# Masking ahead of the exponential: a top-k attention and two gated layers on one core

## The chip, the cores and the metric

The kernel runs on one NeuronCore of a Trainium2 chip. The metric is the device time of one execution in microseconds. Five engines share the work: PE (TensorE, matrix products), DVE (VectorE), ACT (ScalarE), POOL (GpSimd) and SP (SyncE, which here only issues DMAs). Each runs its own list of instructions strictly in order, and semaphores join the lists.

## The reference

The input is q, k and v of 4 batches x 8 heads x 576 tokens x 64, and four weight matrices of 512 x 2048 or 2048 x 512, which come as 64-bit floats.

```
scores = q @ k^T / 8                                  # 576 x 576 for each head
kth    = the 32nd largest score of each row
scores = where(scores >= kth, scores, -1e9)
attn   = exp(scores - max(scores)); attn = attn / (sum(attn) + 1e-9)
x      = attn @ v, heads side by side                 # 2304 tokens x 512
h      = max(x @ w_in1, 0);  y = (h * h) @ w_out1
h      = y @ w_in2;          out = (h * clip(h + 3, 0, 6) / 6) @ w_out2
```

## The kernel before, in words

Matrix operands are split into two 16-bit halves, a high and a low one, and a product is the sum of three 16-bit products (high-high, high-low, low-high). So most steps come as a pair: ACT copies the high half, POOL or DVE subtracts it to get the low half.

**Attention.** The queries of a batch are cut into blocks: four of 128 tokens, and one of 64 whose heads go in pairs. A block has 8 tiles (one for a head), the short one 4, 144 in all. In `attend` a tile goes through: `qk` on PE (128 x 576 scores in PSUM); `evac`, ACT, to `S` in SBUF; `topk`, seven instructions on DVE: MAX8 gives the 8 largest of a row, MATCH_REPLACE8 strikes them out into a copy `W`, and so on, until `m` holds the 32 largest; `bias` on POOL (scale times the maximum, negated); `expo` on ACT, `E` = exp(scale * S + bias), which needs only the first MAX8; `mask` on DVE, one instruction that multiplies `E` by (S >= 32nd value) and also adds up the row; `high` on ACT and `low` on POOL, which fill `wc`; `flip`, a DMA transpose from `wc` to `wT`, issued by SP; `av` on PE, which multiplies `wT` with the values.

**From a block to a unit.** When a block's tiles are done, `x_operand` divides by the row sums, transposes on PE and splits the result into the operand buffer `hl`. A unit is 128 tokens (a full block, or two short ones): 18 units. For each, `group` runs eight steps for either layer: 4 x 12 products into `hb` (`up`), ACT and DVE for the nonlinearity, ACT `high` and POOL `low` into `ghl`, then products into `acc`. The second layer of a unit needs all of its first layer.

**Weights.** SP loads 67 pieces of the four matrices; DVE turns the 64-bit words into 32-bit floats (`conv`), ACT and POOL add low bits, PE and DVE find a scale from the whole matrix (`gram`, `maxes`), and PE, ACT and POOL split the scaled pieces. The first layer's products wait for the scales and pieces of matrices 0 and 1.

**What sets the order.** `Plan` holds every step as a task with an engine, a cost in microseconds, a key, its predecessors and the buffers it takes. It plays the program through: an engine that is free takes the ready task with the lowest key whose buffers are free; a task's successors become ready its cost plus a latency later (`LAT`; 2.0 for SP). The order in which tasks start there is the order of each engine's instructions. Keys are pairs: a class, then a position. The classes are the constants at the end of the file: `AKEY` (attention on ACT and POOL), `GKEY` (the layers on ACT and POOL), `CKEY`, `WKEY`, `SKEY`, `SPL` (weights), `XKEY`, `PREP`, `QKV`. Buffer counts are the numbers given to `pool`.

Of the kernel before, what the change touches and what calls it, by code (L numbers as in the profile page):

```python
# [32 lines left out]
class Plan:  # L33
# [99 lines left out]
def tile_topk_attention_moe_moe2(  # L133
# [79 lines left out]
    acc_t = ps.tile([P, 2, 512], F32, name="acc")  # L213
    plan.pool(acc0=1, acc1=1)
    pool("S", SBUFS, [P, S], F32)
    pool("W", 2, [P, S], F32)
    pool("E", 2, [P, S], F32)
    pool("wc", 2, [P, 2 * S], F16)
    pool("wT", 2, [P, 2 * S // P, P], F16)
# [17 lines left out]
    scalar("wmx", 4)
# [349 lines left out]
    def norm_tasks(tag, src, junk, n, cost, deps, alloc, inv, kkey, reads=(), writes=()):  # L587

        box = {}

        def square():
            for a_ in alloc:
                T[a_, kkey] = take(a_)
            box["ss"] = take("ss")
            nc.scalar.activation(junk(), src(), AF.Square, accum_out=box["ss"][0:n])

        def total():
            box["pn"] = take("misc", "pn" + tag)
# [88 lines left out]
    def q_prep(i, half):  # L687
# [63 lines left out]
    def attend(s):  # L751
# [87 lines left out]
        for r in range(7):  # L839
# [8 lines left out]
        tm = task("DVE", 0.815, (2, s + 0.7), mask, port=True, deps=[ops[6], te, mask_task.get((i, 0))],  # L848
                  alloc=["sums"] if t == 0 else [])
        mask_task[i, t] = tm  # L850
        free("S", tb, tm)
        free("m", ops[0], tm)
        th = task("ACT", 0.57, (AKEY[2], s), high, deps=[tm, before[2]], alloc=["wc"])
        tl = task("POOL", 1.38, (AKEY[3], s), low, deps=[th, before[3]])
        free("E", te, tl)
# [425 lines left out]
SPL = (3.5, 1.5, 0.5)
ADD = (0.5, 1)
PREP = 1.5
VKEY = 3

CKEY = ((-3.61, 0.14), (-69.99, 3.36), (-31.64, 0.91), (-0.36, 1.29))
SKEY = (0, 100, 200, 300)
# [27 lines left out]
```

## Time and profile before

| | |
|---|---|
| median of 3 runs | 1236.63 us (1236.08 to 1240.48) |
| the profiled execution | 1238.58 us, span 1236.8 us, 36708 instructions |
| PE busy | 1074.3 us, 87% of the span |
| DVE busy | 1058.9 us, 86% |
| ACT busy | 825.4 us, 67% |
| POOL busy | 663.8 us, 54% |
| granted TensorE clock, mean | 0.947 |

The span runs from the first instruction to the last; the 1.8 us by which the execution is longer lie around it. Busy time is the union of an engine's instructions. An instruction's mean duration includes its way through the engine, and the next one may start before it ends; so what an instruction costs its engine is best read from start to start, where a timeline shows it.

### The profile page before, as it was taken

To read this page: it belongs to the slowest core of one execution; us is meant where nothing else is said; L and a number is where in the kernel's file an instruction comes from. 1 tells how busy PE (TensorE), PEld (TensorE's weight loads), DVE (VectorE), ACT (ScalarE), POOL (GpSimd) and SP (SyncE) were. 2 spreads that over 40 slices of the span, in tenths; PEclk is the share of its full clock that TensorE was granted. 3 is DMA by queue.
4 is the path that set the end of the run, shared out by engine and by line. 5 is a ranking of instruction groups with operands and counts; after the bars stand their busy time and mean duration, and the time that the engine had idled before them with its cause. 6 is when DMAs were issued, how large, how long until landed. Compare 5 with 4: busy or idle time off the path is not lost.

```text
span 1236.8 us, 36708 instructions
## 1 busy us (share of the span) xinstructions
PE 1074.3 (87%) x14856; PEld 879.4 (71%) x14856; DVE 1058.9 (86%) x2463; ACT 825.4 (67%) x1580; POOL 663.8 (54%) x969
## 2 busy tenths in 40 slices
PE   2484389878989999999899999999998999999998
PEld 2332147577679769877887888788767868978885
DVE  5999999999978999999999999999868989999011
ACT  7677588769767668666766757576866666755422
POOL 5857846458654556554545555655544555545312
PEclk9676599998999999999899999999998999999999
DMA  9989744333454233344574323435433233433100
GB/s 209 268 247 265 228 101 115 71 55 55 96 113 93 53 63 70 66 71 82 89 109 72 68 56 71 55 64 98 97 59 73 54 66 73 65 49 58 22 2 18
DMA packets 276762, 112.47 MB, mean 91 GB/s; under 512 B 257521, under 2 KB 265713, under 8 KB 276593
## 3 DMA queue, kind: packets, MB, share of 16 engines
q1 hardware_dynamic: 276592, 110.14, 43.3%
q8 instruction: 116, 1.90, 0.6%
q14 instruction: 54, 0.43, 0.1%
HBM read 48.23 MB, written 4.72 MB: 43 GB/s over the span
## 4 chain that ended last, share of the span: by engine, by line
PE 42%; DVE 15%; ACT 10%; DMA 10%; issue 5%; POOL 5%; SPq 1%; POOLq 0%; DVEq 0%; ACTq 0%
PE hb L1075 16%; PE acc L1118 9%; PE acc L1110 8%; DMA wT<-wc 8%; DVE W L783 4%; DVE m L786 4%; PE av L829 3%; PE sp L764 3%; DVE E L801 2%; DVE m L778 2%; POOL wc L810 1%; ACT E L795 1%; POOL ghl L1100 1%; ACT x L896 1%; ACT S L770 1%
## 5 line engine op out<-in xcount | busy, mean ns | idle before, releaser
L1075 PE MATMUL hb<-hl,w 128*128 128x128 f16 x6912 | 455.8, 220 | 3.7 <-ACT r L1082 2.2
L1075 PEld LDWEIGHTS <-w 128*128 128x128 f16 x6912 | 415.7, 99 | 42.8 <-issue 6.2
L786 DVE MAX8 m<-W 128x8 f32<-128x576 f32 x432 | 314.8, 747 | 0.2
L1100 POOL TENSOR_TENSOR ghl<-r,ghl 128x512 f16<-128x512 f32 x144 | 172.7, 1201 | 193.3 <-ACT ghl L1097 141.9
L1110 PE MATMUL acc<-ghl,w 128*128 128x128 f16 x3456 | 242.0, 221 | 9.9 <-POOL ghl L1100 4.2
L810 POOL TENSOR_TENSOR wc<-E,wc 128x512 f16<-128x512 f32 x144 | 167.8, 1165 | 145.2 <-ACT wc L806 117.8
L1118 PE MATMUL acc<-w,ghl 128*128 128x512 f16 x864 | 234.3, 382 | 2.8 <-POOL ghl L1100 1.5
L1110 PEld LDWEIGHTS <-w 128*128 128x128 f16 x3456 | 212.8, 99 | 29.8 <-issue 14.0
L783 DVE MATCH_REPLACE8 W<-m,W 128x576 f32<-128x576 f32 x288 | 213.3, 742 | 0.0
L795 ACT ACTIVATE E<-S,scalars,scl 128x576 f32<-128x576 f32 x144 | 124.8, 867 | 85.9 <-POOL scalars L790 65.3
L801 DVE SCALAR_TENSOR_TENSOR E<-S,m,E 128x576 f32<-128x576 f32 x144 | 137.2, 952 | 0.1
L770 ACT ACTIVATE S<-sp 128x576 f32<-128x576 f32 x144 | 92.9, 645 | 53.8 <-DVE E L801 40.9
L764 PE MATMUL sp<-kT,qT 128*128 128x288 f16 (+1 forms) x640 | 102.4, 303 | 25.0 <-ACT S L770 21.0
L829 PE MATMUL av<-vv,wT 128*128 128x64 f16 (+1 forms) x2240 | 92.7, 197 | 33.7 <-DMA wT<-wc 32.8
L829 PEld LDWEIGHTS <-wT 128*128 128x128 f16 (+1 forms) x2240 | 81.2, 103 | 56.5 <-DMA wT<-wc 46.9
L1097 ACT ACTIVATE ghl<-r 128x512 f16<-128x512 f32 x144 | 89.8, 626 | 40.9 <-PE acc L1110 21.2
L778 DVE MAX8 m<-S 128x8 f32<-128x576 f32 x144 | 107.3, 746 | 4.9 <-ACT S L770 4.9
L783 DVE MATCH_REPLACE8 W<-m,S 128x576 f32<-128x576 f32 x144 | 106.8, 741 | 0.0
L1118 PEld LDWEIGHTS <-ghl 128*128 128x128 f16 x864 | 73.8, 99 | 45.2 <-issue 3.3
L806 ACT ACTIVATE wc<-E 128x576 f16<-128x576 f32 x144 | 97.7, 679 | 4.6 <-DVE E L801 4.5
L412 POOL TENSOR_TENSOR w<-w,stg 128x512 int32<-128x512 int32 x57 | 73.0, 1294 | 35.4 <-DVE w L365 23.6
L1090 DVE SCALAR_TENSOR_TENSOR r<-r,hb 128x512 f32<-128x512 f32 x72 | 48.9, 680 | 49.6 <-ACT r L1084 49.4
(128 smaller groups left out, 1343.2 us busy)
## 6 DMA issues: line engine op xcount, KB each, us to landing
w<-in_moe_w_in_dram SPq DMA_DIRECT2D x32, 512.0 KB, 4.8
w<-in_moe_w_out_dram SPq DMA_DIRECT2D x29, 512.0 KB, 4.8
out_dram<-o SPq DMA_DIRECT2D x16, 256.0 KB, 2.4
qf<-in_q_dram SPq DMA_DIRECT2D x31, 128.0 KB, 3.1
stg<-in_k_dram SPq DMA_DIRECT2D x12, 256.0 KB, 3.2
stg<-in_v_dram SPq DMA_DIRECT2D x12, 256.0 KB, 3.1
wT<-wc SPq DMA_TRANSPOSE x144, 3.2
stg<-in_moe_w_out_dram SPq DMA_DIRECT2D x6, 256.0 KB, 3.9
```

The source lines that it names most:

```text
L764: nc.tensor.matmul(dst, qT[:, 2 * ((2 * hp + hh) % 4) + a, 0:M], kflat[:, hh * SPAD + c * HALF:hh * SPAD + (c + 1) * HALF], start=a == 0, ...
L778: nc.vector.max(m[:, 0:8], T["S", s])
L783: nc.vector.match_replace(out=T["W", s], in_to_replace=m[:, 8 * c - 8:8 * c], in_values=T["S", s] if c == 1 else T["W", s], imm_value=-3.0e38)
L786: nc.vector.max(m[:, 4 * r:4 * r + 8], T["W", s])
L795: nc.scalar.activation(T["E", s], T["S", s], AF.Exp, bias=T["nb", s], scale=T["scl", ("q", i, half)][:, hp % 2:hp % 2 + 1])
L801: nc.vector.scalar_tensor_tensor(T["E", s], T["S", s], T["m", s][:, TOPK - 1:TOPK], T["E", s], op0=ALU.is_ge, op1=ALU.mult, accum_out=T["s ...
L810: nc.gpsimd.tensor_tensor(wc[:, S + TAIL:], e[:, 0:S - TAIL], wc[:, 0:S - TAIL], op=ALU.subtract)
L829: nc.tensor.matmul(out_[cols, t * D:(t + 1) * D], wT[0:kr, a, cols], vv[0:kr, vb, hh, c, :], start=n_ == 0, stop=n_ == len(prods) - 1)
L1075: nc.tensor.matmul(box["h"][:, fi * n:(fi + 1) * n], wt[2 * m][:, kk * 4 + f // 4, a, f % 4 * P:(f % 4 + 1) * P], hl[:, c, kk, 0:n], start ...
L1100: nc.gpsimd.tensor_tensor(flat(box["g"][:, 1]), flat(box["r"]), flat(box["g"][:, 0]), op=ALU.subtract)
L1110: nc.tensor.matmul(flat_[:, c * w_:c * w_ + n], wt[1][:, f, a, c * P:(c + 1) * P], gl[d], start=(f, a, d) == (0, 0, 0) and c * w_ % 512 == ...
L1118: nc.tensor.matmul(o_, gl[d][:, ch * P:ch * P + rows], wt[3][:, f, a, :], start=f == 0 and (a, d) == (0, 0), stop=f == KF - 1 and (a, d) = ...
```

## The change

The mask moves. After `topk`, DVE computes one value for each row, `kb` = 32nd value x 2^96. ACT then writes `E` = relu(kb - 2^96 * S), which is zero for a kept score and huge for another. POOL subtracts, `E` = S - E. The exponential runs on `E` and adds up the row itself (`accum_out`). DVE's masking instruction is gone. `S` is now freed by POOL's subtraction, `E` is held from the relu to `low`, and the exponential waits for the whole of `topk`. The factor 1/8 moves into the q scale, and `scl` is bounded from below.

The buffers: `W` 2 to 1, `m` 3 to 4, `nb` 2 to 3, `hl` from 2 of 256 columns to 4 of 128 (the same bytes). SP's transposes of `wc` get a planned latency of 3.5 us instead of 2.0. Nearly all keys get new numbers; the layers' classes on ACT and POOL go from 4 and 1.5 to 29.26 and 27.97, which is behind the attention's.

```diff
-    pool("W", 2, [P, S], F32)
+    pool("W", 1, [P, S], F32)
-    pool("hl", 2, [P, 2, KD, 2 * P], F16)
+    pool("hl", HBUFS, [P, 2, KD, P], F16)
-    pool("m", 3, [P, TOPK], F32, st)
+    pool("m", 4, [P, TOPK], F32, st)
...
+        def lowest():
+            T["kb", s] = take("kb")
+            nc.vector.tensor_scalar(T["kb", s], T["m", s][:, TOPK - 1:TOPK], FAR, None, op0=ALU.mult)
+        def below():
+            T["E", s] = take("E")
+            nc.scalar.activation(T["E", s], T["S", s], AF.Relu, bias=T["kb", s], scale=-FAR)
+        def mask():
+            nc.gpsimd.tensor_tensor(T["E", s], T["S", s], T["E", s], op=ALU.subtract)
         def expo():
-            T["E", s] = take("E")
-            nc.scalar.activation(T["E", s], T["S", s], AF.Exp, bias=T["nb", s],
-                                 scale=T["scl", ("q", i, half)][:, hp % 2:hp % 2 + 1])
-        def mask():
             if t == 0:
                 T["sums", i] = take("sums")
-            nc.vector.scalar_tensor_tensor(T["E", s], T["S", s], T["m", s][:, TOPK - 1:TOPK], T["E", s],
-                                           op0=ALU.is_ge, op1=ALU.mult, accum_out=T["sums", i][:, t:t + 1])
+            nc.scalar.activation(T["E", s], T["E", s], AF.Exp, bias=T["nb", s],
+                                 scale=T["scl", ("q", i, half)][:, hp % 2:hp % 2 + 1],
+                                 accum_out=T["sums", i][:, t:t + 1])
...
-        te = task("ACT", 0.76, (AKEY[1], s), expo, deps=[tn, before[1]], alloc=["E"])
+        tk = task("DVE", 0.07, (2, s + 0.7), lowest, deps=[ops[6]], alloc=["kb"])
+        tr = task("ACT", 0.68, (AKEY[1], s), below, deps=[tk, before[1]], alloc=["E"])
+        tm = task("POOL", 1.24, (MKEY, s), mask, deps=[tr])
+        free("S", tb, tm)
+        te = task("ACT", 0.96, (AKEY[1], s), expo, deps=[tn, tm, mask_task.get((i, 0))], ...)
-        tm = task("DVE", 0.815, (2, s + 0.7), mask, port=True, deps=[ops[6], te, mask_task.get((i, 0))], ...)
-        tw = task("SP", 1.25, (0, s), flip, deps=[tl, before[4]], alloc=["wT"])
+        tw = task("SP", 1.25, (0, s), flip, deps=[tl, before[4]], alloc=["wT"], lat=WLAT)
...
-GKEY = (4, 1.5)
-AKEY = (0.5, 1, 3, 3.5)
+GKEY = (29.26, 27.97)
+AKEY = (0.09, 1, 4.41, 4.29)
-WKEY = ((45.68, 1), (153.74, 0.1), (14.48, 0.1), (62.46, 0.1))
+WKEY = ((36.97, 0.2), (83.47, 1.54), (106.39, 0.2), (97.4, 0.05))
```

On DVE, in the middle of the program, two tiles took turns in the top-k steps before (the numbers behind W and m are one tile's buffers):

```order
L783 MATCH_REPLACE W_10658<-m_10625,S_10361 128x576
L783 MATCH_REPLACE W_10486<-m_10359,W_10486 128x576
L786 MAX m_10625<-W_10658 128x8
L786 MAX m_10359<-W_10486 128x8
L783 MATCH_REPLACE W_10658<-m_10625,W_10658 128x576
L1090 SCALAR_TENSOR_TENSOR r_10687<-r_10687,hb_10547 128x512
L801 SCALAR_TENSOR_TENSOR E_10457,sums_10319<-S_10252,m_10359,E_10457 128x576
```

Now, at about the same tile, one tile goes through alone, and line 795 stands for the mask:

```order
L795 TENSOR_SCALAR scalars_85<-m_10291 128x1
L783 MATCH_REPLACE W_10656<-m_10485,S_10440 128x576
L786 MAX m_10485<-W_10656 128x8
L783 MATCH_REPLACE W_10656<-m_10485,W_10656 128x576
L1101 SCALAR_TENSOR_TENSOR r_10690<-r_10690,hb_10525 128x512
L786 MAX m_10485<-W_10656 128x8
L783 MATCH_REPLACE W_10656<-m_10485,W_10656 128x576
L786 MAX m_10485<-W_10656 128x8
```

With one `W`, an instruction of DVE now mostly reads what the one just ahead of it wrote. In the whole list, DVE has 12 such neighbours among the top-k steps and what follows them before, and 503 now: 232 times a MAX behind its own MATCH_REPLACE (6 before), 184 times a MATCH_REPLACE behind its own MAX (5 before), 87 times line 795 behind its own MAX.

On POOL, a stretch in the second half of the program before (wc is a tile's low half, ghl that of a layer's step):

```order
L790 TENSOR_SCALAR scalars_85<-m_11415,scl_10321 128x1
L279 TENSOR_TENSOR kn_11346<-qf_10988,kn_11346 128x4x64
L810 TENSOR_TENSOR wc_11413<-E_11195,wc_11413 128x512
L811 TENSOR_TENSOR wc_11413<-E_11195,wc_11413 128x64
L279 TENSOR_TENSOR kn_11346<-qf_10988,kn_11346 128x4x64
L1100 TENSOR_TENSOR ghl_11510<-r_11475,ghl_11510 128x512
L1100 TENSOR_TENSOR ghl_11570<-r_11526,ghl_11570 128x512
```

And a like stretch now:

```order
L803 TENSOR_TENSOR E_11630<-S_11345,E_11630 128x576
L966 TENSOR_TENSOR hl_11481<-y_11551,hl_11481 128x512
L1111 TENSOR_TENSOR ghl_11677<-r_11646,ghl_11677 128x512
L790 TENSOR_SCALAR scalars_85<-m_11719,scl_10844 128x1
L818 TENSOR_TENSOR wc_11737<-E_11630,wc_11737 128x512
L819 TENSOR_TENSOR wc_11737<-E_11630,wc_11737 128x64
L803 TENSOR_TENSOR E_11773<-S_11463,E_11773 128x576
```

Each tile has one more wide instruction on POOL (line 803), which stands between the steps of the layers; the low half of a tile comes four rows behind its own subtraction, with ACT's exponential and copy in between.

On SP, the loads around the last pieces of matrix 1 (in_moe_w_out) before, where matrix 2 (in_moe2_w_in) and 3 (in_moe2_w_out) are mixed in:

```order
L343 DMA w3_89<-in_moe2_w_in_dram 128x1024 x2
L343 DMA w2_88<-in_moe_w_out_dram 128x1024
L725 DMA_TRANSPOSE qT_960<-kn_959 128x8x128
L343 DMA w3_89<-in_moe2_w_in_dram 128x1024 x2
L703 DMA qf_1094<-in_q_dram 128x4x64
L343 DMA w3_89<-in_moe2_w_out_dram 128x1024
L343 DMA w2_88<-in_moe_w_out_dram 128x1024 x2
L343 DMA w3_89<-in_moe2_w_out_dram 128x1024
```

And now:

```order
L343 DMA w2_88<-in_moe_w_out_dram 128x1024 x3
L823 DMA_TRANSPOSE wT_859<-wc_815 128x9x128
L343 DMA w2_88<-in_moe_w_out_dram 128x1024 x2
L823 DMA_TRANSPOSE wT_905<-wc_882 128x9x128
L343 DMA w3_89<-in_moe2_w_in_dram 128x1024
L343 DMA w2_88<-in_moe_w_out_dram 128x1024
L343 DMA w3_89<-in_moe2_w_in_dram 128x1024
L823 DMA_TRANSPOSE wT_1001<-wc_964 128x9x128
L343 DMA w3_89<-in_moe2_w_in_dram 128x1024 x4
```

The last piece of matrix 1 was the 50th weight load of SP and is now the 33rd; pieces of matrices 2 and 3 moved behind it.

## Rows read from the trace of the kernel before

**Rows 1.** The page: busy us of each engine, share of the span, instructions

```profile
PE 1074.3 (87%) x14856; PEld 879.4 (71%) x14856; DVE 1058.9 (86%) x2463; ACT 825.4 (67%) x1580; POOL 663.8 (54%) x969
```

**Rows 2.** Busy time by stretch: length, then each engine, granted clock, DMA share, GB/s

```profile
0.00:180.00 180.00, 93.83 (x546) 53.15 (x547) 157.25 (x340) 125.34 (x233) 118.56 (x146) 0.75 0.82 225
180.00:300.00 120.00, 101.40 (x1384) 83.08 (x1382) 115.33 (x273) 95.48 (x184) 69.97 (x104) 0.94 0.39 74
300.00:1150.00 850.00, 798.99 (x11857) 678.06 (x11855) 776.59 (x1828) 574.02 (x1110) 456.19 (x703) 0.98 0.41 73
1150.00:1237.00 87.00, 80.12 (x1080) 65.08 (x1078) 9.69 (x25) 30.51 (x55) 19.05 (x18) 0.99 0.04 12
```

**Rows 3.** PE's waits, 300 to 1237 us: in total, times, longest

```profile
PE av L829 <- DMA wT<-wc: 26.6, 25, 2.3
```

**Rows 4.** The tile wT: its transposes from issue to landing

```profile
DMA to landing us min/median/max: 3.2/3.2/5.1
```

**Rows 5.** DVE's mask, line 801, by stretch; the group of a 128x1 instruction

```profile
0.00:1237.00 1237.00, 138.34 (x288) 0.95 0.44 91
...
300.00:1150.00 850.00, 111.38 (x230) 0.98 0.41 73
...
L262 DVE TENSOR_SCALAR scalars<-scalars 128x1 int32<-128x1 int32 x114 | 17.5, 153 | 4.2
```

**Rows 6.** Timeline of DVE, the last tile alone: start us, duration us, instruction

```profile
1138.68 0.80 DVE L801 SCALAR_TENSOR_TENSOR E<-S,m,E 128x576 f32<-128x576 f32 x1
...
1139.48 0.74 DVE L783 MATCH_REPLACE8 W<-m,W 128x576 f32<-128x576 f32 x1
1140.26 0.76 DVE L786 MAX8 m<-W 128x8 f32<-128x576 f32 x1
...
1141.13 0.74 DVE L783 MATCH_REPLACE8 W<-m,W 128x576 f32<-128x576 f32 x1
1141.91 0.76 DVE L786 MAX8 m<-W 128x8 f32<-128x576 f32 x1
1142.78 0.82 DVE L801 SCALAR_TENSOR_TENSOR E<-S,m,E 128x576 f32<-128x576 f32 x1
```

**Rows 7.** Timeline of DVE, two tiles in turn

```profile
1031.92 0.74 DVE L786 MAX8 m<-W 128x8 f32<-128x576 f32 x1
...
1032.64 0.74 DVE L783 MATCH_REPLACE8 W<-m,S 128x576 f32<-128x576 f32 x1
1033.30 0.08 DVE L783 MATCH_VALUE_LOAD W<-m,W 128x8 f32 x1
```

**Rows 8.** Groups of ACT and POOL: busy us, mean ns, idle before

```profile
L810 POOL TENSOR_TENSOR wc<-E,wc 128x512 f16<-128x512 f32 x144 | 167.8, 1165 | 145.2 <-ACT wc L806 117.8 <-DVE m L778 15.3 <-issue 5.6
L795 ACT ACTIVATE E<-S,scalars,scl 128x576 f32<-128x576 f32 x144 | 124.8, 867 | 85.9 <-POOL scalars L790 65.3 <-POOL wc L811 20.3
L806 ACT ACTIVATE wc<-E 128x576 f16<-128x576 f32 x144 | 97.7, 679 | 4.6 <-DVE E L801 4.5
L412 POOL TENSOR_TENSOR w<-w,stg 128x512 int32<-128x512 int32 x57 | 73.0, 1294 | 35.4 <-DVE w L365 23.6 <-ACT stg L408 6.1 <-DVE scalars L466 2.3
L811 POOL TENSOR_TENSOR wc<-E,wc 128x64 f16<-128x64 f32 x144 | 50.2, 349 | 0.0
L595 ACT ACTIVATION_READ_ACCUMULATOR kn<-qf 128x1 f32 (+1 forms) x39 | 7.6, 194 | 0.0
```

**Rows 9.** Timeline of DVE: matrix 1's maximum; the last block's row sums

```profile
145.39 0.68 DVE L362 TENSOR_SCALAR cv<-w 128x512 int32<-128x512 int32 x1
145.99 0.68 DVE L365 SCALAR_TENSOR_TENSOR w<-w,cv 128x512 int32<-128x512 int32 x1
146.58 0.68 DVE L448 TENSOR_REDUCE scalars<-acc 128x1 f32<-128x512 f32 x1
...
1143.64 0.17 DVE L880 TENSOR_SCALAR rv<-sums 128x8 f32<-128x8 f32 x1
```

**Rows 10.** Timeline of PE: the first product of the layers

```profile
179.41 0.83 PE L1075 MATMUL hb<-hl,w 128*128 128x128 f16 x12
```

More of the change, by code (lines that the diff above doesn't have):

```diff
@@ L215, in tile_topk_attention_moe_moe2 @@
     pool("S", SBUFS, [P, S], F32)
-    pool("W", 2, [P, S], F32)
+    pool("W", 1, [P, S], F32)
     pool("E", 2, [P, S], F32)
     pool("wc", 2, [P, 2 * S], F16)
-    pool("wT", 2, [P, 2 * S // P, P], F16)
+    pool("wT", WTB, [P, 2 * S // P, P], F16)
     pool("kn", 1, [P, 4 * NCH * D], F16)
@@ L233, in tile_topk_attention_moe_moe2 @@
     pool("scl", 3, [P, 2], F32, st)
-    for name, n in (("nb", 2), ("ss", 6), ("sck", 1), ("scv", 1), ("scq", 2), ("qinv", 2), ("xy", 2), ("scx", 6),
+    for name, n in (("nb", NBUFS), ("kb", 2), ("ss", 6), ("sck", 1), ("scv", 1), ("scq", 2), ("qinv", 2), ("xy", 2), ("scx", 6),
                     ("px", 6), ("sc2", 4), ("p2", 2), ("r", 6), ("pm", 2), ("sm", 2), ("ca", 2), ("oc", 2)):
@@ L602, in scale @@
             box["sc"] = take("sc" + tag)
-            scale_pair(box["pn"][:, 0:1], inv(), EXP_I, box["sc"])
+            scale_pair(box["pn"][:, 0:1], inv(), EXP_I - (3 << 23) * (tag == "q"), box["sc"])
         t1 = task("ACT", cost, (PREP, when(kkey)), square, deps=deps, alloc=["ss", *alloc], reads=reads, writes=writes)
@@ L721, in scales @@
                 nc.gpsimd.tensor_scalar(T["scl", kkey][:, c:c + 1], kvinv[:, 0, b % 2, hp:hp + 1],
-                                        T["qinv", kkey][:, 0:1], 0.125, op0=ALU.mult, op1=ALU.mult)
+                                        T["qinv", kkey][:, 0:1], SCLMIN, op0=ALU.mult, op1=ALU.max)
         def flip():
@@ L844, in attend @@
         tn = task("POOL", 0.25, (0, s), bias, deps=[ops[0], scl_use[i, half][0]], alloc=["nb"])
-        te = task("ACT", 0.76, (AKEY[1], s), expo, deps=[tn, before[1]], alloc=["E"])
+        tk = task("DVE", 0.07, (2, s + 0.7), lowest, deps=[ops[6]], alloc=["kb"])
+        free("m", ops[0], tk, tn)
+        tr = task("ACT", 0.68, (AKEY[1], s), below, deps=[tk, before[1]], alloc=["E"])
+        free("kb", tk, tr)
+        tm = task("POOL", 1.24, (MKEY, s), mask, deps=[tr])
+        free("S", tb, tm)
+        te = task("ACT", 0.96, (AKEY[1], s), expo, deps=[tn, tm, mask_task.get((i, 0))],
+                  alloc=["sums"] if t == 0 else [])
         free("nb", tn, te)
         scl_use[i, half][1].append(te)
[L848 to L853, printed above, removed]
+        mask_task[i, t] = te
+        th = task("ACT", 0.57, (AKEY[2], s), high, deps=[te, before[2]], alloc=["wc"])
         tl = task("POOL", 1.38, (AKEY[3], s), low, deps=[th, before[3]])
-        free("E", te, tl)
-        tw = task("SP", 1.25, (0, s), flip, deps=[tl, before[4]], alloc=["wT"])
+        free("E", tr, tl)
+        tw = task("SP", 1.25, (0, s), flip, deps=[tl, before[4]], alloc=["wT"], lat=WLAT)
         free("wc", th, tw)
@@ L860, in attend @@
         av_tasks[i, t] = tv
-        tile_tasks.append((ta, te, th, tl, tw, tv))
+        tile_tasks.append((ta, tr, th, tl, tw, tv))
         free("wT", tw, tv)
@@ L1265 @@
 XBUFS = 1
+HBUFS = 4
 GBUFS = 3
@@ L1271 @@
 SQ0 = 'a'
-GKEY = (4, 1.5)
-AKEY = (0.5, 1, 3, 3.5)
+GKEY = (29.26, 27.97)
+AKEY = (0.09, 1, 4.41, 4.29)
 SX = 'a'
 SX0 = 'a'
-XKEY = 1.5
+XKEY = 37.4
 NPOOL = (4, 4, 4, 4)
-QKV = 0
-WKEY = ((45.68, 1), (153.74, 0.1), (14.48, 0.1), (62.46, 0.1))
+QKV = 4.45
+WKEY = ((36.97, 0.2), (83.47, 1.54), (106.39, 0.2), (97.4, 0.05))
 SPE = ('eeee', 'eeee', 'eeea', 'aaaa')
[L1281 to L1287, printed above, removed]
+SPL = (2.26, 0.06, 0.05)
+ADD = (-0.97, 0.86)
+PREP = 1.04
+VKEY = 27.33
+MKEY = -0.5
+WLAT = 3.5
+WTB = 2
+NBUFS = 3
+FAR = 2.0 ** 96
+SCLMIN = 2.0 ** -56
+CKEY = ((-3.23, 0.38), (-66.39, 4.6), (-35.42, 1.77), (-0.72, 1.02))
+SKEY = (0.99, 124.56, 208.36, 272.85)
 _INS = ["q", "k", "v", "moe_w_in", "moe_w_out", "moe2_w_in", "moe2_w_out"]
```

## The prediction

> **What bounds the kernel now.** I read the busy times first: PE 87%, DVE 86%, ACT 67%, POOL 54% [rows 1]. Two engines are nearly full and the other two have room; the change takes work from one of the full ones and gives it to the two with room. Then the stretches [rows 2], since an average hides stages. From 0 to 180 us PE is busy 93.8 us, so 86.2 are idle: this is the stage of weights, with DVE at 157.3 of 180 and DMA at 0.82. The layers' first product starts at 179.4 [rows 10], 33 us behind the maximum of matrix 1 at 146.6 [rows 9]. From 180 to 300, PE's idle time is 18.6 us; from 300 to 1150 it is 51.0 with DVE at 776.6 of 850 (91%); in the last 87 us it is 6.9 and DVE has nothing left. These four make 162.7, and 1074.3 + 162.7 = 1237. So there are two limits at once: PE must do its 1074 us, and DVE must finish the last block (1143.6, [rows 9]) before the last 93 us can run. Third, PE's waits: in the 57.9 us that PE is idle after 300, 26.6 are one wait, `av` for the transposed `wT` [rows 3]. A transpose takes 3.2 to 5.1 us to land [rows 4], and the plan of before counts 2.0, so its order puts `av` a little too early, 25 times.
>
> **DVE: the mask goes.** Line 801 holds DVE for 138.3 us, its accumulator reads included [rows 5], of which a part overlaps the next instruction: undisturbed it is 0.73 + 0.07 us from start to the next work (1138.68 to 1139.48, [rows 6]), 144 x 0.80 = 115. I take 127, between the two.
>
> **DVE: line 795 comes.** 144 instructions on one value a row. A like one is 153 ns long [rows 5], so 22 us is the upper end; pipelined behind independent work it would be about half. I take 10; zero is the lower end.
>
> **DVE: one `W`.** With two tiles in turn, MATCH_REPLACE8 to the next instruction is 0.66 us (1032.64 to 1033.30) and MAX8 to the MATCH_REPLACE8 proper 0.72 (1031.92 to 1032.64) [rows 7]. In the one tile that ran alone at the end these are 0.78 (1139.48 to 1140.26) and 0.87 (1140.26 to 1141.13), and MAX8 to the mask, which reads its result, 0.87 against 0.66 [rows 6]. So an instruction that reads what its neighbour has just written costs 0.12, 0.15 or 0.21 us more. The new order has 226, 179 and 86 more such neighbours: 226 x 0.12 + 179 x 0.15 + 86 x 0.21 = 27 + 27 + 18 = 72 us. This is the price of the buffer that the change gives up, and it shows nowhere in DVE's busy time. Its lower end is zero, if other waits cover it; its upper end is 503 x 0.21 = 106. DVE's net is thus -127 + 10 + 72 = -45 us, with ends -138 and +13 (-115 + 22 + 106).
>
> The Trainium skill says otherwise here: on its page "VectorE: DVE Perf Modes", section "The DRAIN you can't avoid", a chain of VectorE instructions costs the same with a semaphore after each as with one after the last. This trace disagrees, by the 0.12 to 0.21 us above. By that rule the 72 us would not be there and DVE's net would be -117; that is a rival below.
>
> **ACT.** The relu over 128x576 is new. Its neighbours are the copy of line 806 (679 ns, no operand per row) and the exponential of line 795 before (867 ns, two such operands) [rows 8]; relu has one, so 0.77, and 144 x 0.77 = 111 us, ends 98 and 125. The exponential's sum adds an accumulator read of 194 ns [rows 8]: 28 us. Together 139: ACT goes from 825 to about 964, 80% of a span of 1206. From 300 to 1150 there are 115 tiles (230 instructions of line 801, two for a tile, [rows 5]), one in 7.4 us: 574 + 115 x 0.96 = 684 of 850, 81%. There is room, but queues get longer. From 180 to 300 ACT already has 95.5 of 120 [rows 2]; 0.96 us for each of 16 tiles make it 111, 92%. There ACT is nearly the bound, and I charge 2 us of PE idle time to it.
>
> **POOL.** The subtraction is 576 wide. From the low half of 512 columns (1165 ns) it would be 1.31 us, from the 32-bit addition of line 412 (1294 ns) 1.46 [rows 8]. 144 x 1.31 = 189, ends 168 (no more than the 512 columns cost) and 210. POOL goes from 664 to about 853, 71%. Neither engine becomes the bound by its sum.
>
> **PE.** Its instructions are the same in number and kind. What changes is when they can run.
> First stage: ahead of the maximum of matrix 1, DVE has 20 conversion steps fewer (0.68 us long, about 0.6 from start to start [rows 9]: -12), 9 masks fewer (-8), and pays some 28 neighbour stalls (+4); so the maximum comes about 15 us sooner on DVE's account, and the matrix's last piece is SP's 33rd load and not the 50th. But the split that follows runs on ACT, which has more to do ahead of it: one more tile of evacuation and nine relus and sums. I count 8 us of gain, ends 20 and -4.
> After 300: the plan now waits 3.5 us for a transpose. In the new order the layers' products that stand between a tile's `qk` and its `av` are worth some 34 us of PE's work, counted over all tiles, and not 32. The chain behind top-k grows by about 3 us (relu, subtraction and exponential 0.77 + 1.31 + 1.06 come, the mask's 0.8 goes, two hand-overs more), while a tile alone is through DVE's seven steps in 4 x 0.66 + 3 x 0.72 + 3 x 0.12 + 3 x 0.15 = 5.6 us, and two in turn take 9.6 for both. So `av` has 2 - 3 + 4 = 3 us more room, and I let 22 of the 26.6 us go. Four `hl` buffers instead of two let the attention run further ahead of the layers, which covers some of the small gaps; from the other 31 us I take 3. The rest stays.
> Sum on PE's side: 1074.3 busy + (86.2 - 8) + (18.6 + 2) + (57.9 - 25) = 1206.
>
> DVE's side must agree: 1143.6 - 45 = 1099 for the last block. Behind the last `av`, PE has 768 + 336 products of 128 columns left and not 636 + 288 as before, 1.19 times as many; the last 87 us with 80.1 busy [rows 2] become about 87 + 15 = 102, plus the 6 between the row sums and that window. 1099 + 108 = 1207. The two sides meet within a microsecond, so neither is slack, and I forecast a span of 1206. The execution is 1.8 us longer than its span and the profiled run lies 2.0 above the median of before (1238.58 against 1236.63), so as a median 1206.
>
> **Rivals.**
> First, slower: the two `E` buffers. Before, `E` is held over the exponential, mask, copy and low half. Now it is held over relu 0.77, subtraction 1.31, exponential 0.87 + 0.19, copy 0.68 and low half 1.17 + 0.35 = 5.3 us of work [rows 8] plus five hand-overs between ACT and POOL, each behind whatever stands in line. 850 us for 115 tiles is 7.4 us a tile, so two buffers allow a hold of 14.8: 1.9 us per hand-over. At 2.0 us, the hold is 15.3 and a tile takes 7.65: 0.25 x 115 = 29 us more, and with 8 gained early 1237 + 29 - 8 = 1258. For it: ACT at 81% and POOL at 71%, each with instructions of about a microsecond in line, and the layers' work now stands last in their classes, so that PE starves first. Against it: the waits on `ghl` are small today and POOL idles 145 us ahead of line 810 [rows 8].
> Second, nothing happens: DVE's stalls and line 795 come at their upper ends, the net is about zero, the last block stays at 1143, and PE's saved waits for `wT` only turn into waits for the next block. With 4 us from the first stage this is 1233. For it: the bounds above include it.
> Third, no stall between neighbours, as if rows 6 held for the program's end alone. DVE's net is -117, DVE ends at about 1027 and is no limit any more. PE keeps 75 + 16 us idle before 300 and, with its wait on `wT` and half of the rest gone, 16 after: 1074.3 + 107 = 1181. For it: little but that rows 6 are few; against it, all three kinds of neighbours in [rows 6] show the stall.
> The Trainium skill's section named above would have this rival too; the trace is against it, by [rows 6].
>
> **How the numbers follow.** 0.5% of 1236.6 is 6.2 us, so faster means below 1230, slower above 1243. The forecast, 1192 to 1222 on its own: chance 0.60, all faster. The third rival 0.13, faster. The second 0.13: most within 0.5%, 0.03 of it below 1230. The first 0.14, of which 0.01 ends within 0.5%. That makes faster 0.76, same 0.11, slower 0.13. The range of 1176 to 1243 leaves out the first rival and the far end of the third.
>
> **What would show it.** DVE's busy time falls to about 945 while its last block ends only some 45 us sooner; from start to start its top-k steps read 0.78 and 0.87. ACT near 964 and POOL near 853. PE's wait for `wT` after 300 falls below 8 us. Matrix 1's maximum comes before 140 and the first product before 175. Wrong would be: PE's waits for `ghl` or `hb` of tens of microseconds, relus that wait for line 819 (the first rival), a DVE without stalls that ends before 1050 (the third), or a last block at 1140 (the second).

## The result, and the profile after

The changed kernel takes 1205.74 us (median of 4 runs, 1203.63 to 1206.85) against 1238.56 (4 runs, 1236.08 to 1240.84): a ratio of 0.9733, 95% interval 0.9706 to 0.9761. The profiled execution took 1205.79 us, its span 1204.0, the mean granted clock of TensorE 0.968 (0.947 before). That difference in clock is not the gain: 17 further executions of the kernel before, with a granted clock of 0.964 to 0.967, have a median of 1235.9 us, less than 3 us below 1238.56. The prediction was 1206, faster.

The page's busy times, which answer to [rows 1]:

```profile
PE 1072.1 (89%) x14856; PEld 879.2 (73%) x14856; DVE 991.3 (82%) x2319; ACT 929.2 (77%) x1868; POOL 833.8 (69%) x1113
```

DVE has 68 us less, ACT 104 more, POOL 170 more. The same four stretches as in [rows 2]; the last is shorter, since the program is:

```profile
0.00:180.00 180.00, 106.56 (x632) 59.86 (x633) 152.98 (x344) 139.68 (x273) 133.27 (x163) 0.90 0.74 210
180.00:300.00 120.00, 94.53 (x1259) 77.09 (x1258) 112.11 (x264) 101.47 (x205) 91.52 (x119) 0.90 0.44 97
300.00:1150.00 850.00, 824.46 (x12424) 707.85 (x12424) 719.84 (x1700) 674.25 (x1370) 599.24 (x824) 0.99 0.40 74
1150.00:1204.00 54.00, 46.55 (x546) 34.42 (x543) 6.33 (x13) 13.80 (x22) 9.81 (x10) 0.99 0.03 11
```

Length less PE's busy time is PE's idle time: 73.4 us in the first stage (86.2 before), 25.5 in the second (18.6), and 25.5 + 7.5 = 33.0 after 300 (57.7 before, to the end of its span at 1236.8). 1072.1 + 131.9 = 1204. PE's waits after 300 us, the longest sum and the one of [rows 3]:

```profile
PE sp L764 <- ACT S L770: 8.9, 14, 4.6
...
PE av L837 <- DMA wT<-wc: 1.5, 3, 0.8
```

The 25 waits for a transpose have become three. Now DVE, one tile alone in mid-program, which answers to [rows 6] and [rows 7] (start us, duration us, instruction):

```profile
1005.43 0.74 DVE L786 MAX8 m<-W 128x8 f32<-128x576 f32 x1
1006.21 0.15 DVE L795 TENSOR_SCALAR scalars<-m 128x1 f32<-128x1 f32 x1
1006.28 0.08 DVE L783 MATCH_VALUE_LOAD W<-m,S 128x8 f32 x1
1006.35 0.74 DVE L783 MATCH_REPLACE8 W<-m,S 128x576 f32<-128x576 f32 x1
1007.13 0.76 DVE L786 MAX8 m<-W 128x8 f32<-128x576 f32 x1
1007.92 0.09 DVE L783 MATCH_VALUE_LOAD W<-m,W 128x8 f32 x1
1008.00 0.74 DVE L783 MATCH_REPLACE8 W<-m,W 128x576 f32<-128x576 f32 x1
1008.78 0.76 DVE L786 MAX8 m<-W 128x8 f32<-128x576 f32 x1
```

From start to start, MATCH_REPLACE8 to its own MAX8 is 0.78 us (1006.35 to 1007.13), MAX8 to its own MATCH_REPLACE8 0.87 (1007.13 to 1008.00), MAX8 to line 795 0.78 (1005.43 to 1006.21). The groups that the change made, with line 818 as the old line 810 (busy us, mean ns, idle before; [rows 8]):

```profile
L803 POOL TENSOR_TENSOR E<-S,E 128x576 f32<-128x576 f32 x144 | 203.7, 1415 | 42.6 <-ACT E L800 41.6 <-PE av L837 0.5
L818 POOL TENSOR_TENSOR wc<-E,wc 128x512 f16<-128x512 f32 x144 | 167.9, 1166 | 55.5 <-ACT wc L814 54.7
```
```profile
L808 ACT ACTIVATE E<-E,scalars,scl 128x576 f32<-128x576 f32 x144 | 124.2, 863 | 2.9 <-POOL E L803 2.8
...
L808 ACT ACTIVATION_READ_ACCUMULATOR E<-E,scalars,scl 128x1 f32 x144 | 28.1, 195 | 0.0
...
L795 DVE TENSOR_SCALAR scalars<-m 128x1 f32<-128x1 f32 x144 | 21.5, 149 | 3.0
```

The new relu of line 800 stands beside them at 774 ns. Last the three marks: on DVE the maximum of matrix 1 and the last block's row sums [rows 9], on PE the first product of the layers [rows 10]:

```profile
128.16 0.69 DVE L448 TENSOR_REDUCE scalars<-acc 128x1 f32<-128x512 f32 x1 [0.23 <-PE acc L428]
...
1091.24 0.15 DVE L795 TENSOR_SCALAR scalars<-m 128x1 f32<-128x1 f32 x1
...
1095.02 0.17 DVE L891 TENSOR_SCALAR rv<-sums 128x8 f32<-128x8 f32 x1
1095.23 0.20 DVE L892 RECIPROCAL rv<-rv 128x8 f32<-128x8 f32 x1
```
```profile
166.05 0.83 PE L1086 MATMUL hb<-hl,w 128*128 128x128 f16 x12 [0.21 <-DVE w L365]
```

The row sums now come from ACT: DVE's own part of the last block is over with line 795 at 1091.4, and the mark at 1095 stands 3.6 us behind it. Before, DVE wrote the sums itself, and the mark followed at once.

### The profile page after: what moved, and what is told of

Its sections match the earlier page's. It is cut to its first block, busy times and chain, and to the rows that moved or that the text cites. A ratio compares the mean times of both kernels' runs of the same rounds, so it can differ in the third digit from the quotient of the medians.

```text
span 1204.0 us, 37051 instructions
## 1 busy us (share of the span) xinstructions
PE 1072.1 (89%) x14856; PEld 879.2 (73%) x14856; DVE 991.3 (82%) x2319; ACT 929.2 (77%) x1868; POOL 833.8 (69%) x1113
## 4 chain that ended last, share of the span: by engine, by line
PE 39%; DVE 22%; ACT 17%; POOL 11%; issue 5%; DMA 4%; SPq 1%; POOLq 0%; ACTq 0%; DVEq 0%
PE hb L1086 15%; PE acc L1129 10%; PE acc L1121 7%; DVE W L783 6%; DVE m L786 6%; POOL E L803 4%; PE sp L764 3%; DVE m L778 2%; POOL wc L818 2%; ACT E L808 2%; ACT S L770 2%; PE av L837 2%; ACT x L907 1%; ACT E L800 1%; DVE cv L362 1%
## 5 line engine op out<-in xcount | busy, mean ns | idle before, releaser
L1086 PE MATMUL hb<-hl,w 128*128 128x128 f16 x6912 | 461.3, 220 | 3.7 <-DVE r L1101 1.1
L786 DVE MAX8 m<-W 128x8 f32<-128x576 f32 x432 | 325.9, 754 | 7.9
L1111 POOL TENSOR_TENSOR ghl<-r,ghl 128x512 f16<-128x512 f32 x144 | 166.9, 1161 | 120.5 <-ACT ghl L1108 112.8
L803 POOL TENSOR_TENSOR E<-S,E 128x576 f32<-128x576 f32 x144 | 203.7, 1415 | 42.6 <-ACT E L800 41.6
L1121 PEld LDWEIGHTS <-w 128*128 128x128 f16 x3456 | 211.2, 99 | 18.2 <-issue 4.8
L818 POOL TENSOR_TENSOR wc<-E,wc 128x512 f16<-128x512 f32 x144 | 167.9, 1166 | 55.5 <-ACT wc L814 54.7
L800 ACT ACTIVATE E<-S,scalars 128x576 f32<-128x576 f32 x144 | 111.5, 774 | 28.4 <-DVE scalars L795 27.3
L808 ACT ACTIVATE E<-E,scalars,scl 128x576 f32<-128x576 f32 x144 | 124.2, 863 | 2.9 <-POOL E L803 2.8
L1129 PEld LDWEIGHTS <-ghl 128*128 128x128 f16 x864 | 73.8, 98 | 46.7 <-issue 5.5
L764 PEld LDWEIGHTS <-qT 128*128 128x128 f16 (+1 forms) x640 | 56.9, 105 | 61.6 <-issue 40.9
L1095 ACT ACTIVATE r<-hb,bias,scalars 128x512 f32<-128x512 f32 x72 | 55.8, 775 | 54.1 <-PE hb L1086 52.3
```

What stands on the lines that cost most here:

```text
L764: nc.tensor.matmul(dst, qT[:, 2 * ((2 * hp + hh) % 4) + a, 0:M], kflat[:, hh * SPAD + c * HALF:hh * SPAD + (c + 1) * HALF], start=a == 0, ...
L786: nc.vector.max(m[:, 4 * r:4 * r + 8], T["W", s])
L800: nc.scalar.activation(T["E", s], T["S", s], AF.Relu, bias=T["kb", s], scale=-FAR)
L803: nc.gpsimd.tensor_tensor(T["E", s], T["S", s], T["E", s], op=ALU.subtract)
L808: nc.scalar.activation(T["E", s], T["E", s], AF.Exp, bias=T["nb", s], scale=T["scl", ("q", i, half)][:, hp % 2:hp % 2 + 1], accum_out=T["s ...
L818: nc.gpsimd.tensor_tensor(wc[:, S + TAIL:], e[:, 0:S - TAIL], wc[:, 0:S - TAIL], op=ALU.subtract)
```

## The experiments

A number that comes out right doesn't show that its reasons were. The prediction's theory was two limits at once: PE's work with its waits, and DVE's end. The rivals: PE alone decides, with what it waits for, and DVE's relief does little; the new order of the weights and layers does it, not the mask; and, after the first results, the fit of the plan: how well one particular order happens to mesh.

In the table below, idle is PE's, by stretch; the last block is the start of RECIPROCAL for its row sums. Ratios are to the kernel before on the same chip (1237.2, 1238.2 and 1237.6 us in the three groups of runs). PE's busy time differs by up to 18 us between the runs, though all have the same number of products, 14,856; so PE's time does not divide cleanly into busy and idle.

| kernel | us | ratio (95%) | PE busy | idle 0-180, 180-300, after | last block | first layer product |
|---|---|---|---|---|---|---|
| before | 1238.6 | 1 | 1074.3 | 86.2, 18.6, 57.7 | 1143.8 | 179.4 |
| after | 1205.7 | 0.973 (0.971-0.976) | 1072.1 | 73.4, 25.5, 33.0 | 1095.2 | 166.1 |
| old_plan_latency | 1229.3 | 0.994 (0.991-0.996) | 1070.4 | 94.4, 16.3, 46.2 | 1133.7 | 225.3 |
| old_mask_moved | 1247.8 | 1.008 (1.005-1.011) | 1080.4 | 84.1, 31.7, 49.9 | 1113.8 | 224.6 |
| new_mask_on_dve | 1232.9 | 0.996 (0.994-0.998) | 1086.8 | 71.4, 22.3, 50.4 | 1131.5 | 155.6 |
| new_two_w | 1225.8 | 0.991 (0.987-0.994) | 1077.8 | 74.1, 18.2, 53.5 | 1056.4 | 168.4 |
| new_dve_less | 1204.1 | 0.971 (0.968-0.975) | 1069.9 | 72.9, 26.0, 31.3 | 1091.4 | 164.7 |
| new_dve_more | 1233.8 | 0.995 (0.992-0.997) | 1084.9 | 73.8, 23.3, 50.0 | 1121.4 | 167.3 |
| old_dve_less | 1235.8 | 0.998 (0.996-1.001) | 1068.9 | 85.7, 19.7, 57.4 | 1137.8 | 180.3 |
| new_jitter_relu | 1227.2 | 0.990 (0.987-0.993) | 1075.9 | 75.6, 17.8, 58.2 | 1114.1 | 200.2 |
| new_jitter_pool | 1218.6 | 0.983 (0.980-0.987) | 1074.5 | 76.5, 17.0, 49.9 | 1092.8 | 199.2 |
| old_jitter_exp | 1235.1 | 0.997 (0.995-1.000) | 1073.3 | 87.8, 12.8, 59.5 | 1134.7 | 185.2 |
| old_low_short | 1220.7 | 0.985 (0.982-0.989) | 1072.5 | 84.6, 17.5, 46.4 | 1127.4 | 177.4 |
| old_low_and_dve | 1217.6 | 0.982 (0.977-0.987) | 1069.8 | 85.6, 17.6, 43.4 | 1121.5 | 179.2 |

### One part of the change at a time

**old_plan_latency**: the kernel before, with the transpose's planned latency alone.

```diff
-        tw = task("SP", 1.25, (0, s), flip, deps=[tl, before[4]], alloc=["wT"])
+        tw = task("SP", 1.25, (0, s), flip, deps=[tl, before[4]], alloc=["wT"], lat=3.5)
```

> The kernel before with the one planned latency of the wT transposes raised from 2.0 to 3.5 us. Theory (two limits: PE's idle time and DVE's last block both had to fall): PE's wait for wT after 300 us falls below 10 of 26.6 us, but DVE still ends its last block at 1143 +- 8, so the time is 1228 to 1240. Rival (the wait for wT was the gain, the mask beside the point): 25 us less, 1207 to 1216.

Measured: 8 us faster, in the theory's range; the last block came 10 us sooner, a little more than the 8 that the theory allowed. The wait for `wT` after 300 us falls to a single one of 1.0 us, but PE's idle time there only from 57.7 to 46.2; what PE now waits for longest is the layers' low halves:

```profile
PE acc L1110 <- POOL ghl L1100: 9.9, 7, 2.7
...
PE av L829 <- DMA wT<-wc: 1.0, 1, 1.0
```

So a wait of 26.6 us that goes takes less than half of that off PE's idle time there, since part returns as other waits; and 8 us are lost in the first stage, where this plan puts the first layer product at 225.

**old_mask_moved**: the new computation and its `W`, `m` and `nb` buffers, with all planning numbers, the latency and the `hl` buffers of before.

```diff
-HBUFS = 4
-GKEY = (29.26, 27.97)
-AKEY = (0.09, 1, 4.41, 4.29)
+HBUFS = 2
+GKEY = (4, 1.5)
+AKEY = (0.5, 1, 3, 3.5)
...
-WLAT = 3.5
+WLAT = 2.0
```

> The mask moved to ACT and GpSimd with one W buffer, but with the keys, the two hl buffers and the 2.0 us latency of the kernel before. Theory: DVE's last block ends near 1100, the waits for wT stay at 20 to 35 us, and since PE now is the nearer limit about half of the gain shows: 1215 to 1232. Rival (the mask's move alone brings the gain): 1203 to 1212. Second rival (the longer chain hurts without the new keys): 1240 or more.

Measured: 10 us slower than before, though the last block is 30 us sooner. The theory's 1215 to 1232 missed; the time lies in the second rival's range. PE still waits for the transpose, if a little less than the 20 us at least that the theory said:

```profile
PE av L837 <- DMA wT<-wc: 18.7, 22, 3.4
```

In this order, then, relieving DVE bought nothing. Whether the longer chain behind top-k cost the 10 us, as the second rival has it, or the order, is not told apart.

**new_mask_on_dve**: the new planning numbers, latency and `hl` buffers, with the mask on DVE and two `W` as before.

```diff
-    pool("W", 1, [P, S], F32)
+    pool("W", 2, [P, S], F32)
...
-        tm = task("POOL", 1.24, (MKEY, s), mask, deps=[tr])
+        tm = task("DVE", 0.815, (2, s + 0.7), mask, port=True, deps=[ops[6], te, mask_task.get((i, 0))], ...)
```

> The changed kernel with the mask back on DVE (two W buffers): new keys, four hl buffers and the 3.5 us latency stay. Theory: waits for wT after 300 us below 8 us, matrix 1's maximum still near 130, but DVE's last block near 1140, so 1222 to 1238. Rival (keys, buffers and latency bring the gain alone): 1203 to 1212.

Measured: 4 us faster than before, in the theory's range, with PE's wait for `wT` after 300 us at 2.3 us. It has the whole gain of the first stage (PE idle 71.4, the first product at 155.6), with the mask still on DVE; old_mask_moved has hardly any of it (84.1). In the table, all seven kernels with the new numbers have 71 to 77 us there, the seven with the old ones 84 to 94. So that gain goes with the new planning numbers, and with the `hl` buffers and latency that came with them, but not with the mask. The weights' order is the likely part, since the maximum of matrix 1 comes at 118 us here and at 143 in old_mask_moved; no run has it alone. And it is not the first layer product that brings it: new_jitter_relu and new_jitter_pool (below) have it with that product at 199 to 200 us. The latency (-8), the numbers and buffers with it (-4) and the mask (+10) don't add up to the change's -33.

**new_two_w**: the change with the second `W` kept.

```diff
-    pool("W", 1, [P, S], F32)
+    pool("W", 2, [P, S], F32)
```

> The changed kernel with two W buffers again: DVE has 40 neighbours that wait for each other and not 503. Theory: DVE's stalls of 0.12 to 0.15 us go (about 60 us of its time), its last block ends 20 to 50 us sooner, but PE holds the end: 1188 to 1206. Rival (DVE's chain is still the limit): 1165 or less. Second rival (two tiles in flight run short of S and E): 1206 or more.

Measured: 40 neighbours that read each other instead of 503, and DVE's busy time is 945.8 us, not 991.3. The last block's row sums:

```profile
1056.39 0.20 DVE L892 RECIPROCAL rv<-rv 128x8 f32<-128x8 f32 x1
```

That is 39 us before those of the change, and yet the kernel is 20 us slower: the theory's 1188 to 1206 missed. An earlier end of DVE's part does not by itself make the program shorter. (Another buffer count is also another order, see below: the 20 us can't be put down to `W`, nor to the second rival's shortage of `S` and `E`.)

### DVE by itself, in a fixed order

These three keep every engine's planned order, instruction by instruction, and change only what DVE takes for a tile. Two shorten an instruction: a MAX8 over 288 columns takes 449 ns and not 757. The third adds one.

**new_dve_less**, on the change, and **old_dve_less**, on the kernel before:

```diff
-                nc.vector.max(m[:, 4 * r:4 * r + 8], T["W", s])
+                nc.vector.max(m[:, 4 * r:4 * r + 8], T["W", s][:, 0:288] if r == 6 else T["W", s])
```

> The changed kernel with every engine's order unchanged, but the last MAX8 of a tile looks at 288 of 576 columns (part of the top-k is left out): DVE has 0.30 us a tile less, 43 us in all. Theory now, after the two-W run (in the changed kernel PE alone is the limit): the time stays within 5 us of 1205.7. Rival, as the prediction had it (DVE's and PE's sides meet, neither is slack): DVE's last block 15 us or more sooner and the time unchanged or some us less, 1195 to 1203.

> The kernel before, order unchanged, with the same half MAX8 (part of the top-k left out): DVE has 43 us less, as much as the change took off it, and nothing else differs. Theory (two limits): PE's waits for wT and its small gaps stay in its order, so most of the 43 us turn into idle time of DVE: 1222 to 1236. Rival (DVE was the limit, the gain is DVE's): 1195 to 1210.

Measured: 144 x 0.31 = 44 us less of DVE's work (38 and 44 of its busy time) is worth 1.6 us in the one and 2.3 in the other, at the edge of what can be told. Both theories held. The last block comes 4 and 6 us sooner, not 44:

```profile
1091.36 0.20 DVE L892 RECIPROCAL rv<-rv 128x8 f32<-128x8 f32 x1
```

The time went into DVE's waits. Between 300 us and the end of the last top-k, DVE is idle for 68.4 us in the kernel before and 99.4 in old_dve_less, 77.6 in the change and 107.4 in new_dve_less. The two largest groups of old_dve_less, from 300 to 1150 us; in the kernel before they are 19.0 and 10.8 us:

```profile
DVE r L1090 <- ACT r L1084: 27.5, 27, 3.1
...
DVE scalars L261 <- PE pnq L599: 21.4, 17, 3.2
```

DVE comes sooner to instructions that PE and ACT are not ready for, and waits. In a list strictly in order, an engine at 91% can be paced by others all the same.

**new_dve_more**: one MAX8 over 288 columns more for each tile, ahead of line 795.

```diff
             T["kb", s] = take("kb")
+            nc.vector.max(junk8, T["W", s][:, 0:288])
```

> The changed kernel, order unchanged, with one more MAX8 over 288 columns a tile on DVE (result unused): 0.37 us and perhaps a wait for its neighbour of 0.1, so 53 to 70 us more, which is what the change took off DVE. If DVE is just below being the limit: the last block comes 30 to 60 us later and the time is 1220 to 1245. If DVE has slack of its own (PE alone the limit): 1206 to 1214.

Measured: 144 x 445 ns = 64 us more, 48 in DVE's busy time, cost 28, of which 13 stand in PE's busy time (1084.9 us against 1072.1). The last block comes 26 us later, less than the 30 expected, and ACT's relu waits 43.3 us for the row's value from 300 to 1150, against 22.0 in the change:

```profile
ACT E L802 <- DVE scalars L797: 43.3, 53, 3.2
```

So less work on DVE gives next to nothing and more work costs. That DVE then is the limit is not shown: it is still idle for 62 us between 300 us and the end of the last top-k, and the instruction also puts line 795 0.24 us later behind the tile's last MAX8 (median 1.04 against 0.80 us). Which of the two costs the 28 us, this run does not tell.

### The plan by itself

**new_jitter_relu**, **new_jitter_pool** and **old_jitter_exp**: the same instructions with the same buffers; one planned cost is 0.01 us higher, which makes the plan another order.

```diff
-        tr = task("ACT", 0.68, (AKEY[1], s), below, deps=[tk, before[1]], alloc=["E"])
+        tr = task("ACT", 0.69, (AKEY[1], s), below, deps=[tk, before[1]], alloc=["E"])
```
```diff
-        tm = task("POOL", 1.24, (MKEY, s), mask, deps=[tr])
+        tm = task("POOL", 1.25, (MKEY, s), mask, deps=[tr])
```
```diff
-        te = task("ACT", 0.76, (AKEY[1], s), expo, deps=[tn, before[1]], alloc=["E"])
+        te = task("ACT", 0.77, (AKEY[1], s), expo, deps=[tn, before[1]], alloc=["E"])
```

> The changed kernel with the relu's planned cost 0.69 instead of 0.68 us: nothing in the work changes, only which ready step goes first, and the orders of PE and DVE differ in thousands of places. It measures how far the time hangs on the plan alone. If little: 1202 to 1209, and then the two-W run's 20 us are W's. If the numbers of the file fit just this plan: 1212 to 1230, and then a run that plans anew can't price a part to better than that.

> The changed kernel with the subtraction's planned cost on POOL 1.25 instead of 1.24 us: again nothing in the work changes, only ties in the plan. If the changed kernel's plan is one good draw among many: 1215 to 1232. If the first of these two was the unlucky one: 1202 to 1210.

> The kernel before with the exponential's planned cost 0.77 instead of 0.76 us, nothing else. If its numbers fit its plan as the changed kernel's fit theirs: 1242 to 1260. If its plan is an ordinary draw: 1230 to 1245.

Measured: the changed kernel becomes 21 and 13 us slower, the old one 2 us faster: the ranges for a plan that happens to fit, and for an ordinary one. Much of the loss stands in one place. The stretch from 300 to 350 us, of the change:

```profile
300.00:350.00 50.00, 44.72 (x572) 33.11 (x572) 41.77 (x99) 42.50 (x90) 42.94 (x59) 0.88 0.59 107
```

and of new_jitter_pool, with its two largest PE waits in that stretch:

```profile
300.00:350.00 50.00, 30.26 (x420) 23.73 (x421) 32.59 (x72) 41.18 (x84) 38.89 (x51) 0.80 0.37 73
```
```profile
PE av L837 <- DMA wT<-wc: 9.9, 1, 9.9
PE sp L764 <- ACT S L770: 7.1, 2, 6.6
```

PE is idle 19.7 us of 50 there, and 5.3 in the change. That is 14.5 us in one stretch, of an end that is 13.9 us later (spans 1217.9 and 1204.0); 5 us less of idle time before 300 are made up by 2.5 more behind 350 and 2.4 more of busy time. ACT is nearly as busy in both (41.2 and 42.5 us), so it is not ACT's load that differs; two single waits of PE, of 6.6 and 9.9 us, make up most of the 19.7. new_jitter_relu has the same place (18.7 us idle). The three plans of the changed kernel average 1217 us: about 20 better than before is what the same work gave over these three, and 12 more came with the one order of the change itself. The waits for `wT` after 300 us depend on the order as well:

```profile
PE av L829 <- DMA wT<-wc: 16.6, 23, 1.6
```
```profile
PE av L837 <- DMA wT<-wc: 8.7, 3, 7.7
```
```profile
PE av L837 <- DMA wT<-wc: 12.5, 5, 9.9
```

The first is old_jitter_exp, 10 us less than the 26.6 of before for 2 us of time; the others are new_jitter_relu and new_jitter_pool, against 1.5 in the change, and most of each is the one long wait just named. This spread also bounds what the four runs of the first part can tell, since each of them has an order of its own. Their times among each other, 4 to 22 us apart, can't be put down to the edit. Their waits for `wT` and their ends of DVE can only as far as they differ by more than the order alone moves them (10 to 11 us for the waits, 9 to 21 for the ends); their first stages can by more than 3 us, which is what these three runs differ there from their own kernels at most.

### The chain behind top-k, in a fixed order

**old_low_short**: the kernel before, where POOL sets the wide part of the low half to zero instead of subtracting. **old_low_and_dve** adds the shorter MAX8.

```diff
-            nc.gpsimd.tensor_tensor(wc[:, S + TAIL:], e[:, 0:S - TAIL], wc[:, 0:S - TAIL], op=ALU.subtract)
             nc.gpsimd.tensor_tensor(wc[:, S:S + TAIL], e[:, S - TAIL:], wc[:, S - TAIL:S], op=ALU.subtract)
+            nc.gpsimd.memset(wc[:, S + TAIL:], 0.0)
```

> The kernel before, every engine's order unchanged, but POOL fills 512 of the 576 columns of a tile's low half with zeros (that part of the low half is left out), which takes about 0.7 us a tile off the chain that ends in the transpose, and as much off POOL. The chain's share of the prediction: PE's waits for wT after 300 us fall from 26.6 to 8 to 15 us. Theory (the wait was PE's own loss): the time falls by 8 to 18 us, 1219 to 1229. Rival (PE's waits there cover others, DVE sets the pace): 1232 or more.

> The same with the half MAX8 as well (parts of the low half and of the top-k left out), order unchanged: DVE 43 us less and the chain shorter. If the two limits of the prediction held each other, the two together give clearly more than the sum of each alone: 1195 to 1215. If the order itself is the limit, little more than the shorter chain alone: 1217 to 1229.

Measured: 17 us faster, and 20 with DVE's relief added, the first in the theory's range, the second little more than the shorter chain alone, as expected if the order is the limit. The instructions are now

```profile
L811 POOL MEMSET wc<- 128x512 f16 x144 | 75.5, 524 | 0.0
L810 POOL TENSOR_TENSOR wc<-E,wc 128x64 f16<-128x64 f32 x144 | 44.8, 311 | 155.1 <-ACT wc L806 65.5 <-DVE m L778 41.5 <-issue 8.6
```

0.68 us a tile less (1165 + 349 to 311 + 524 ns), and PE's wait for the transpose after 300 us falls from 26.6 us to 16.0 (8 to 15 were expected) and, with the MAX8, 13.5:

```profile
PE av L829 <- DMA wT<-wc: 16.0, 21, 2.0
```
```profile
PE av L829 <- DMA wT<-wc: 13.5, 18, 1.8
```

So 98 us off POOL, which was 54% busy, gain seven times what 44 us off DVE, 86% busy, do: in this order POOL's step set PE's time, through the chain from top-k to `av` or through POOL's own time, and not the fullest engine beside PE. PE's wait for the transpose fell by 10.6 of the 17 us. Whether the shorter chain alone did it, or POOL's free time gave a part, is not told apart.

## Why the prediction was right, point by point

- **PE's sum.** Predicted -8, +2 and -25 us of PE idle time in the three stretches; measured -12.8, +6.9 and -24.7, and -2.2 busy. The sum held to within 2 us, partly by errors of opposite sign in the first two. That the time agreed to 0.3 us is luck, where a hundredth of a microsecond in the plan moves it by 13 to 21.
- **The first stage.** Maximum and first product came 18 and 13 us sooner (predicted 15 for the maximum; "before 140" and "before 175" held). But the step named the masks as 8 us of the 15, and in new_mask_on_dve, where no mask moved, the maximum comes another 10 us sooner. The gain goes with the new planning numbers; two more orders have it with the first product at 199 to 200 us, so the way from maximum to first product to idle time is not how it came.
- **180 to 300.** 2 us were charged to a full ACT, 6.9 came, with ACT at 101.5 of 120 us (85%) and not 92%. Two other plans of the same work, with ACT as busy (99.2 and 99.7 us), have 17.0 and 17.8 there, no loss at all: an order, not a full engine.
- **After 300.** "I let 22 of the 26.6 us go" and 3 of the rest: 25.1 went of the wait, and next to nothing net of the rest. The latency was the right cause for the wait, and the trace shows how. Tile by tile after 300 us, `av` starts a median of 0.5 us behind the landing of its `wT` in the kernel before and in old_mask_moved, and 1.7 to 1.9 us behind it in old_plan_latency, new_mask_on_dve and the change: the planned latency gives the room, wherever the mask is. (Single long waits can remain: 8.7 and 12.5 us in the change's two other orders.) The prediction's other two terms came true and cancel. From the first MATCH_REPLACE8 of a tile to the end of its top-k the median went from 9.65 to 6.12 us (predicted 9.6 to 5.6), from there to the landing from 8.23 to 11.73 (predicted 3 more). That the idle time followed is not owed to the latency alone: with it alone 11.5 of 57.7 went, with the change in two other orders -0.5 and 7.8. It took an order that fits; what the moved mask has in it is open.
- **DVE's price for one `W`.** Stalls of 0.12 and 0.15 us hold, MAX8 to line 795 costs 0.12 (0.78 against 0.66) and not 0.21: 232 x 0.12 + 184 x 0.15 + 87 x 0.12 = 66 us, against 72. The Trainium skill's rule (page "VectorE: DVE Perf Modes", section "The DRAIN you can't avoid") that a chain costs no more with a semaphore after each instruction, measured there on copies, is not borne out here where each instruction waits for its neighbour's result: 0.78 and 0.87 us against the 0.66 and 0.72 of [rows 7]. "It shows nowhere in DVE's busy time" was wrong: 991.3 against 945.8 with two `W` are 45 us of it, since an instruction that waits for its neighbour starts 0.04 us behind its end (1007.09 to 1007.13), and not 0.08 ahead of it (1033.38 and 1033.30, [rows 7]); and so the sign "falls to about 945" failed. DVE's end came 48.6 us sooner, for 45, and that agreement is luck too: in an unchanged order 44 us less on DVE move its end by 4 to 6.
- **ACT and POOL.** 929 for 964 on ACT: relu and accumulator read have the predicted length (774 and 195 ns), but overlap their neighbours, and 139 us of durations made 104 of busy time. 834 for 853 on POOL, though the subtraction took 1415 ns and not 1310: between the value taken and the upper bound of 1.46. Other groups of POOL took less.
- **The step that failed: "The two sides meet within a microsecond, so neither is slack."** They met, but DVE's side is not a limit: 44 us less on DVE move the end by 2 in either kernel, and new_two_w ends DVE's part 39 us sooner and the program 20 later. In an unchanged order DVE's last block comes where PE and ACT let it come, since 30 us of the relief turn into waits for them. That its end agreed with PE's sum was no second proof: in such an order what stands behind the last block takes the same time (93 to 95 us in the old kernel's four runs, 109 to 111 in the new one's three), so the two ends move as one.
- **What the prediction lacked**: that the time hangs on the plan's order by 13 to 21 us for 0.01 us of a planned cost. Its own range of 1192 to 1222 holds one of the two other plans, not 1227.
- **The rivals.** The second one's mechanism is half true: without the change of the plan, the saved time did turn into other waits (old_mask_moved, old_plan_latency). The first (two `E` buffers) shows no sign: after 300 us PE's largest sum of waits is 8.9 us, and a relu waited for line 819 once, for 0.6 us. The third is refuted by the stalls above and by a last block at 1095 and not near 1027.

What stays open: how the 33 us divide between the moved mask and the fit of its plan. Neither the mask on DVE nor two `W`, with planning numbers fitted to them, was tried.

## What to carry to other kernels

An engine is not shown to be the limit by being the fullest; make its work shorter, in an unchanged order, and see whether the program gets shorter. Two ends that agree in a sum don't prove two limits. Where a planner writes out the order, shift one planned cost by a hundredth of a microsecond and look at the spread before putting a few per cent down to an edit. Give the plan the landing time of a transfer that the trace shows: with a planned 2.0 us for a measured 3.2 PE waited 26.6 us, and planning 3.5 took 25.6 of them away, though only 8 us off the time by itself.

## What the runs showed of the hardware

- An instruction of DVE that reads its neighbour's result starts 0.12 us (MATCH_REPLACE8 to MAX8, MAX8 to a 128x1 instruction) or 0.15 us (MAX8 to MATCH_REPLACE8) later than behind independent work, from start to start a median of 0.78 us over 232 and 87 places of the changed kernel and 0.87 over 184, and the waits show in DVE's busy time (45 us).
- POOL's subtraction took 1415 ns for 576 columns of two 32-bit inputs, and of one 32-bit and one 16-bit input 1166 ns for 512 columns and 323 for 64. A memset of 512 16-bit columns took 524 ns.
- The same DVE instruction can take a quarter longer in one order than in another. The low half of the keys (128x640, line 277), in the change and in new_jitter_pool, with POOL busy for 834 us in both:

```profile
L277 DVE SCALAR_TENSOR_TENSOR kn<-stg,scalars,kn 128x640 f16<-128x640 f32 x12 | 14.4, 1202 | 3.8 <-ACT kn L273 3.8
```
```profile
L277 DVE SCALAR_TENSOR_TENSOR kn<-stg,scalars,kn 128x640 f16<-128x640 f32 x12 | 11.4, 946 | 1.7 <-ACT kn L273 1.6
```

It took 976 ns before, with POOL at 664 us, so POOL's total load is not the reason; what is, was not tested.
